# One attention-and-mixing kernel: a new planner for the work between the score steps, one four-bank score tile with one exp per step, and four small moves

## The chip, the cores and the metric

The kernel runs on one core of one Trainium2 chip. The metric is the device time of one execution in microseconds (us). An execution has a state: fast, or slow when it is over 1.5% above the fastest of the same kernel. A profile is of one execution. The engines are PE (TensorE; PEld is its weight load), ScalarE (ACT), VectorE (DVE), POOL (GpSimd), and SP, whose queue issues nearly all DMAs here.

## The reference

Two attention blocks on the same input of 2048 rows and 640 columns, 32 heads of 20 columns, mixed by a gate per row:

```python
g = sigmoid((x * gate_w).sum(-1))
a = A(x)    # linear attention: q,k -> softmax(+-(q @ w_phi)) features, num/den, @ wo
b = B(x)    # 4 segments of 512 rows: causal softmax attention inside a segment,
            # plus a memory M of the segments before it, mixed by sigmoid(beta), @ wo
return g * a + (1 - g) * b
```

## The kernel before

The first stage (about 97 us) builds the key side of block A and the first segment of block B. Then 32 iterations follow: four segments of eight groups of four heads. An iteration computes scores and exps for one group in three steps (t = 0, 1, 2; 2048, 2048 and 1024 exps per partition), and multiplies the probabilities of the group before with V:

```python
POFF = {0: 0, 1: 512, 3: 896, 2: 1024}
def b_qk(qT, kT, PT, cs):                       # one step
    st2 = [pst.tile([P, 2, 512], F32, name="st") for _ in range(2)]   # 2 x 2 banks, bufs=2
    base = POFF[cs[0]]
    for c in cs:
        ...
        for i in range(4):                      # four heads, 32 rows of the array each
            nc.tensor.matmul(st2[i // 2][:, i % 2, o:o + n], lhsT=kT[...], rhs=qT[...], ...)
    for pr in range(2):
        nc.scalar.activation(out=PT[:, 2 * pr:2 * pr + 2, base:base + w],
                             in_=st2[pr][:, :, 0:w], func=ACT.Exp, scale=SCALE_B)
```

All other work fills PE between these steps as *filler*: projections of the next segment's q, k, v (`b`, `v`), block A's query features (`p`), denominators (`d`) and numerators (`n`), and the output projections (`f`). The kernel is emitted by a planner in Python with a clock of its own: each unit yields the PE time it should take, and `later(dt, f)` emits an instruction dt after. Matmuls run in the order emitted, so a unit placed too early stops everything behind it: in the profile below PE stands 4.40 us before one projection's load, and ScalarE then waits 4.9 us for the scores behind it.

```python
def pick(at):                                   # at: position in iterations
    if BF and BF[0][0] <= at:                   # b, v, f units have a position
        return BF.pop(0)[1]()
    if A3:                                      # p, d, n: whenever nothing else is due
        return A3.pop(0)()
    if BF and BF[0][0] <= at + 1.0:
        return BF.pop(0)[1]()
    return None

ITER = 6.25
PART = (0.38, 0.37, 0.25)
t0 = clock[0]
for k in range(NG):                             # 32 iterations
    at = float(k)
    for t, cs in enumerate(((0,), (1, 3), (2,))):
        now, end = clock[0], t0 + ITER * (at - 0 + PART[t])   # a fixed, absolute timetable
        b_qk(qT, kT, PT, cs)
        while gets and gets[0][0] <= at:
            gets.pop(0)[1]()                    # transposing loads for the projections
        ...
        fill(end, at)
        at += PART[t]
```

An output projection needs its rows transposed. They are stored to DRAM (`od`), loaded transposed (`oT`), multiplied, cast to `osb` and stored to the output. All three DMAs go through SP's queue:

```python
def o_get(s, X, qc, n=KC):
    oT = bw.tile([P, KC, P], BF16, name=f"oT{X}", bufs=5)
    nc.sync.dma_start_transpose(out=oT[:, 0:n], in_=od[s][X][rows, 0:n * P])

def fin_mm(s, qc, hf, X):
    for k5 in range(KC):
        nc.tensor.matmul(sg.ps[:, 0:320], lhsT=sg.oT[qc, X][:, k5, :], rhs=(WoA, WoB)[X][...], ...)
        yield 0.137
    if X:
        nc.vector.tensor_copy(out=sg.osb[...], in_=sg.ps[:, 0:320])
        if hf:
            later(0.6, lambda: nc.sync.dma_start(out=out2[...], in_=osb))
```

The softmax here doesn't subtract the row's maximum and nothing guards it: scores larger than these inputs give would overflow.

## Time and profile before

The median is 378.41 us (four runs, 377.37 to 381.14). The profiled run is the slowest of these, 381.14 us by the run's clock and 379.4 us from first to last instruction. From the starts of the first exp of each iteration in ScalarE's timeline, the profiled 379.4 us split like this:

| stage | us | per iteration |
|---|---|---|
| to the first exp | 97.1 | |
| iterations 0 to 22 | 172.1 | 7.5 |
| iterations 23 to 30 | 82.0 | 10.3 |
| iteration 31 and tail | 28.2 | |

The page of the kernel before: busy tenths of PE in 40 slices of the span, and the clock granted to TensorE in tenths.

```profile
PE   7799998999899998869889899999869665688885
PEclk9999999999999989998899999999987985676597
```

Busy time by window; the columns after the window's length are PE, PEld, VectorE, ScalarE and POOL busy us (instructions), granted clock, DMA share, GB/s.

```profile
229.00:262.00 33.00, 32.42 (x462) 20.94 (x460) 23.81 (x68) 26.93 (x35) 16.73 (x25) 1.00 0.80 182
295.00:328.00 33.00, 20.18 (x239) 11.77 (x236) 13.46 (x36) 14.00 (x18) 17.04 (x28) 0.78 0.58 114
328.00:357.00 29.00, 22.97 (x269) 13.24 (x270) 8.20 (x23) 17.32 (x22) 11.28 (x18) 0.62 0.35 84
```

Where PE is full (229 to 262 us) an iteration takes about 6.6 us; later PE is idle a third of the time and what it does runs at a lower clock. The waits that matter (us in total, times, longest):

```profile
ACT PT L421 <- PE st L415: 66.9, 66, 4.9
PEld L595 <- DMA oT<-od: 13.0, 5, 4.9
PE o_ps L595 <- DMA oT<-od: 11.1, 4, 4.4
PE st L415 <- ACT PT L421: 6.5, 12, 0.9
```

PE's timeline in that stretch (start, us, instruction; idle time before it in brackets):

```profile
313.17 1.44 PE L595 MATMUL o_ps<-WoA,oT 128*128 128x320 bf16 x5 [3.37 <-DMA oT<-od]
319.56 1.25 PE L595 MATMUL o_ps<-WoB,oT 128*128 128x320 bf16 x4 [4.40 <-DMA oT<-od]
323.63 0.84 PE L595 MATMUL o_ps<-WoB,oT 128*128 128x320 bf16 x5
325.97 0.34 PE L415 MATMUL st<-qk 32*128 32x384 bf16 x2 [0.91 <-ACT PT L421]
326.88 0.59 PE L415 MATMUL st<-qk 32*128 32x384 bf16 x6 [0.58 <-ACT PT L421]
329.06 1.52 PE L595 MATMUL o_ps<-WoA,oT 128*128 128x320 bf16 x5 [1.59 <-DMA oT<-od]
```

```profile
295.72 1.42 SPq L401 DMA_TRANSPOSE qk<-qd  x1
302.54 0.33 SPq L604 DMA_DIRECT2D out_dram<-osb  x1
316.69 1.48 SPq L401 DMA_TRANSPOSE qk<-qd  x1
325.10 0.33 SPq L604 DMA_DIRECT2D out_dram<-osb  x1
325.54 2.52 SPq L585 DMA_TRANSPOSE oT<-od  x2
```

Five projection matmuls take 0.84 us at the full clock and 1.5 us after a stretch of waits.

### The profile page before, as it was taken

How to read it: one execution, taken by the hardware profiler on the slowest of the kernel's cores; microseconds unless marked ns; L12 is line 12 of the kernel's file. 1: busy time of each engine (PE TensorE's matmuls, PEld its weight loads, DVE VectorE, ACT ScalarE, POOL GpSimd, SP SyncE). 2: the span in 40 equal slices, each digit the busy share in tenths (PEclk: the TensorE clock that was granted, in tenths of full speed). 3: DMA queues.
4: the chain of work that ended last, by engine and by line, in shares of the span. 5: the costliest groups of instructions: out<-in, count | busy, mean ns of one | idle time of the engine just before them, and what ended most of it. 6: DMA issues, size and time to landing. Idle time of an engine off the chain costs nothing.

```text
span 379.4 us, 9867 instructions
## 1 busy us (share of the span) xinstructions
PE 326.8 (86%) x3999; PEld 210.0 (55%) x4015; DVE 234.8 (62%) x553; ACT 240.7 (63%) x394; POOL 202.7 (53%) x361
## 2 busy tenths in 40 slices
PE   7799998999899998869889899999869665688885
PEld 2577876775465556445556555666535442344462
DVE  1568788777496758666678866877654740233421
ACT  2476665543889868768778788878647452456510
POOL 3149995744484665964445485455564961333500
PEclk9999999999999989998899999999987985676597
DMA  9999200046262432447649487877454557414101
GB/s 187 189 172 363 67 3 2 6 186 175 52 140 86 148 80 97 102 130 173 172 82 192 131 120 218 176 171 137 146 127 146 84 152 136 93 38 118 42 15 56
DMA packets 98327, 46.55 MB, mean 123 GB/s; under 512 B 85482, under 2 KB 96234, under 8 KB 98282
## 3 DMA queue, kind: packets, MB, share of 16 engines
q1 hardware_dynamic: 96304, 45.08, 49.6%
q10 hardware_dynamic: 1978, 0.85, 0.9%
q8 instruction: 31, 0.51, 0.6%
q14 instruction: 14, 0.11, 0.1%
HBM read 4.95 MB, written 20.19 MB: 66 GB/s over the span
## 4 chain that ended last, share of the span: by engine, by line
PE 46%; DVE 19%; ACT 15%; DMA 7%; issue 4%; POOL 4%; SPq 4%; DVEq 0%; ACTq 0%; POOLq 0%
ACT PT L421 8%; PE o_ps L595 7%; PE st L415 7%; PE nd_ps L440 6%; PE qb_ps L230 4%; DVE ksum L262 4%; PE pq_ps L502 4%; PE vb_ps L230 4%; ACT Ek L257 4%; DMA oT<-od 3%; PE kb_ps L230 2%; PE o_ps L780 2%; PE va_ps L230 2%; DVE ts L561 2%; DVE krec L264 2%
## 5 line engine op out<-in xcount | busy, mean ns | idle before, releaser
L421 ACT ACTIVATE PT<-st 128x1024 bf16<-128x1024 f32 (+1 forms) x192 | 159.1, 885 | 68.2 <-PE st L415 66.9
L427 POOL TENSOR_SCALAR_AFFINE_SELECT PT<-PT 128x512 bf16<-128x512 bf16 x128 | 80.1, 640 | 96.3 <-ACT PT L421 96.1
L230 PEld LDWEIGHTS <-xT 128*128 128x128 bf16 x810 | 71.7, 98 | 36.5 <-issue 8.5
L440 PEld LDWEIGHTS <-PT 128*128 128x128 bf16 x1280 | 46.4, 98 | 13.2 <-issue 3.3
L415 PE MATMUL st<-qk 32*128 32x128 bf16 (+3 forms) x512 | 44.8, 326 | 7.6 <-ACT PT L421 6.5
L440 PE MATMUL nd_ps<-vB,PT 128*128 128x21 bf16 x1280 | 47.2, 174 | 0.5 <-DVE dz L525 0.4
L266 POOL TENSOR_TENSOR EkN<-Ek,krec 128x640 bf16<-128x640 bf16 x16 | 25.5, 1593 | 26.0 <-DVE krec L264 26.0
L595 PEld LDWEIGHTS <-oT 128*128 128x128 bf16 x240 | 21.4, 106 | 27.0 <-DMA oT<-od 13.0
L415 PEld LDWEIGHTS <-qk 32*128 32x128 bf16 x512 | 13.7, 93 | 39.1 <-issue 36.3
L502 PE MATMUL pq_ps<-xT,WqA 128*128 128x512 bf16 x84 | 29.3, 411 | 4.1 <-DVE ts L561 1.1
L569 POOL TENSOR_TENSOR oA<-ts 128x320 bf16<-128x320 f32 x32 | 27.6, 874 | 8.8 <-DVE ts L561 8.6
L595 PE MATMUL o_ps<-WoA,oT 128*128 128x320 bf16 x120 | 27.6, 350 | 5.0 <-DMA oT<-od 5.0
L595 PE MATMUL o_ps<-WoB,oT 128*128 128x320 bf16 x120 | 26.4, 328 | 6.2 <-DMA oT<-od 6.1
L475 DVE RECIPROCAL rd<-nd_ps 128x16 f32<-128x16 f32 x32 | 8.1, 254 | 36.9 <-PE nd_ps L440 33.2
L262 DVE TENSOR_REDUCE ksum<-Ek 128x64 f32<-128x1280 bf16 x16 | 23.8, 1485 | 10.8 <-ACT Ek L257 10.8
L556 PE MATMUL num_ps<-KVZ,Eq 128*128 128x140 bf16 (+1 forms) x192 | 20.0, 218 | 12.0 <-DVE stg L383 2.7
L230 PE MATMUL vb_ps<-WvB,xT 128*128 128x320 bf16 x160 | 29.9, 305 | 0.1
L230 PE MATMUL qb_ps<-WqB,xT 128*128 128x320 bf16 x160 | 29.8, 304 | 0.0
L230 PE MATMUL kb_ps<-WkB,xT 128*128 128x320 bf16 x160 | 29.2, 302 | 0.7 <-DVE stg L383 0.7
L257 ACT ACTIVATE Ek<-ka_ps 128x320 bf16<-128x320 f32 x64 | 23.0, 440 | 10.0 <-DVE krec L264 3.6
L561 DVE TENSOR_TENSOR ts<-num_ps,cs 128x320 f32<-128x320 f32 x64 | 27.6, 480 | 2.8 <-POOL cs L546 1.8
L600 DVE CAST osb<-o_ps 128x320 bf16<-128x320 f32 x24 | 11.6, 484 | 26.8 <-PE o_ps L595 26.8
(116 smaller groups left out, 539.2 us busy)
## 6 DMA issues: line engine op xcount, KB each, us to landing
qd<-stg SPq DMA_DIRECT2D x16, 768.0 KB, 3.8
od<-oA SPq DMA_DIRECT2D x16, 160.0 KB, 1.8
out_dram<-osb SPq DMA_DIRECT2D x15, 160.0 KB, 1.9
od<-oB SPq DMA_DIRECT2D x12, 160.0 KB, 1.9
WvA<-in_A_wqkv_dram ACTq DMA_DIRECT2D x2, 400.0 KB, 5.2
WkB<-in_B_wk_dram SPq DMA_DIRECT2D x1, 800.0 KB, 5.4
WqB<-in_B_wq_dram SPq DMA_DIRECT2D x1, 800.0 KB, 7.2
WvB<-in_B_wv_dram SPq DMA_DIRECT2D x1, 800.0 KB, 8.9
```

The lines of the kernel that those rows point to most:

```text
L230: nc.tensor.matmul(ps, lhsT=xT[:, c, sc * P:(sc + 1) * P], rhs=W[:, c, lo:hi], start=(c == 0), stop=(c == KC - 1))
L257: nc.scalar.activation(out=Ek[:, sgn, 320 * hf:320 * hf + 320], in_=ps[:, 0:320], func=ACT.Exp, scale=1.0 if sgn == 0 else -1.0)
L262: nc.vector.tensor_reduce(out=ksum, in_=Ek.rearrange("p s (h f) -> p (s h) f", f=DH), axis=AX.X, op=ALU.add)
L266: eng.tensor_tensor(out=EkNs[sc % 4][:, sgn * D:(sgn + 1) * D].rearrange("p (h f) -> p h f", f=DH), in0=Ek[:, sgn].rearrange("p (h f) -> p ...
L415: nc.tensor.matmul(st2[i // 2][:, i % 2, o:o + n], lhsT=kT[r:r + 32, c * P:(c + 1) * P], rhs=qT[r:r + 32, c * P:L], start=True, stop=True, ...
L421: nc.scalar.activation(out=PT[:, 2 * pr:2 * pr + 2, base:base + w], in_=st2[pr][:, :, 0:w], func=ACT.Exp, scale=SCALE_B)
L427: nc.gpsimd.affine_select(out=view, in_=view, pattern=[[0, 4], [1, P]], compare_op=ALU.is_ge, fill=0.0, base=0, channel_multiplier=-1)
L440: nc.tensor.matmul(nd[:, j * 84 + i * V1:j * 84 + (i + 1) * V1], lhsT=PT[:, i, o:o + P], rhs=vb[:, c, 4 * g + i, :], start=(j == 0 and i = ...
L502: nc.tensor.matmul(ps, lhsT=WqA[:, c, t * P:(t + 1) * P], rhs=xT[:, c, s * L:(s + 1) * L], start=(c == 0), stop=(c == KC - 1))
L561: nc.vector.tensor_tensor(out=ts[:, sgn], in0=ps[:, 0:320].rearrange("p (h e) -> p h e", e=DH), in1=segs[s].cs[hf][:, qc, sgn, :, None].to ...
L569: nc.gpsimd.tensor_tensor(out=oA[:, hf * 320:hf * 320 + 320].rearrange("p (h d) -> p h d", d=DH), in0=ts[:, 0], in1=ts[:, 1], op=ALU.add)
L595: nc.tensor.matmul(sg.ps[:, 0:320], lhsT=sg.oT[qc, X][:, k5, :], rhs=(WoA, WoB)[X][:, k5, hf * 320:hf * 320 + 320], start=(X == 0 and k5 = ...
```

## The change

The intent: keep PE, ScalarE and the DMA queue evenly loaded through all 32 iterations. The diff, cut to its core:

```diff
-        st2 = [pst.tile([P, 2, 512], F32, name="st") for _ in range(2)]
+        st = pst.tile([P, 4, 512], F32, name="st")          # one tile, four banks; bufs=2 -> 1
...
-        for pr in range(2):
-            nc.scalar.activation(out=PT[:, 2 * pr:2 * pr + 2, base:base + w],
-                                 in_=st2[pr][:, :, 0:w], func=ACT.Exp, scale=SCALE_B)
+        nc.scalar.activation(out=PT[:, :, base:base + w], in_=st[:, :, 0:w], func=ACT.Exp,
+                             scale=SCALE_B)
...
-            later(1.0, least)                               # feature map's min, behind its exp
+            later(2.2, least)
-            later(0.5 if s == 0 else 1.0, ...store of qd...)
+            later(0.5 if s == 0 else 2.2, ...)
-            later(1.0, invert)
+            later(1.7, invert)
-            nc.vector.tensor_tensor(out=Mbd[:, g], ...)
+            nc.gpsimd.tensor_tensor(out=Mbd[:, g], ...)
...
     for ic in range(KC):
         run(fold_mm(WkT, WkA, ic))
+        if ic == 2:
+            gate_column()                                   # was after a1_v(1)
...
+    KNOTS_A = ((0, 0.0), (0.37, 8.0), (0.54, 16.0), (0.69, 24.0), (1, 29.6))
+    KNOTS_F = ((0, 10.4), (0.21, 16.0), (0.44, 24.0), (0.64, 27.0), (1, 32.0))
+    # five lists b, v, p, n (with d), f; every unit has a position on these curves
+    def ready(u):
+        if u[0] == "d":   # 1.5 us after its exps
+        if u[0] == "n":   return now > done.get(("d", u[1], u[3]), 1e9) + 5.2
+        if u[0] == "f":   return now > got.get((u[1], u[2], u[4]), 1e9) + 4.5
+        ...
+    def pump(at):         # loads: position reached, data stored 2.2 us ago, a buffer free
...
     def pick(at):         # of the ready heads within 1.6 positions: the latest one,
+        ...               # minus HOLD x the planned backlog of the engines that it loads
...
-    t0 = clock[0]
     for k in range(NG):
+        t0 = clock[0]
+        size = OWN + left() / (NG - k)                      # budget from the work that is left
...
-            now, end = clock[0], t0 + ITER * (at - 0 + PART[t])
+            now, end = clock[0], t0 + size * (at - k + PART[t])
```

Three more `p` units also run before the loop (six instead of three).

More of the change, by code (lines that the diff above doesn't have):

```diff
@@ L74, with use @@
     waiting = []
+    load = {"D": 0.0, "A": 0.0, "G": 0.0, "S": 0.0}
+    def use(**cost):
+        for e, dt in cost.items():
+            load[e] = max(load[e], clock[0]) + dt
     serial = itertools.count()
@@ L388, in b_k @@
                 feature(stg[:, :, 0, :, 0:DH], pk[:, :, :, 0:DH])
-            later(0.5 if s == 0 else 1.0, lambda: nc.sync.dma_start(
+            later(0.5 if s == 0 else 2.2, lambda: nc.sync.dma_start(
                 out=qd[s][c * P:(c + 1) * P, :], in_=stg.rearrange("p g t i e -> p (g t i e)")))
@@ L414, in b_qk @@
                 r = 32 * i
-                nc.tensor.matmul(st2[i // 2][:, i % 2, o:o + n],
+                nc.tensor.matmul(st[:, i, o:o + n],
                                  lhsT=kT[r:r + 32, c * P:(c + 1) * P],
@@ L432, in b_qk @@
         later(1.7 if w > 256 else 1.0, causal)
+        use(A=1.7 if w > 256 else 0.95, G=0.65 * len(cs))
     def b_pv(s, g, PT, js, nd):
@@ L468, in b_mem @@
                                     in1=Msb[:, g], op=ALU.add)
-            nc.vector.tensor_tensor(out=Mbd[:, g], in0=Msb[:, g],
+            nc.gpsimd.tensor_tensor(out=Mbd[:, g], in0=Msb[:, g],
                                     in1=bd4[:, :, None].to_broadcast([P, 4, V1]), op=ALU.mult)
@@ L573, in add @@
                 later(1.0, lambda: o_put(s, 0, qc, oA))
-                if s == NSEG - 1:
-                    later(3.4, lambda: o_get(s, 0, qc))
         later(0.6, add)
+    put, got = {}, {}
     def o_put(s, X, qc, src, w=D):
         nc.sync.dma_start(out=od[s][X][qc * P:(qc + 1) * P, 0:w], in_=src[:, 0:w])
+        put[s, qc, X] = clock[0]
     def o_get(s, X, qc, n=KC):
@@ L586, in o_get @@
         segs[s].oT[qc, X] = oT
+        got[s, qc, X] = clock[0]
     def fin_mm(s, qc, hf, X):
@@ L604, in fin_mm @@
                 later(0.6, lambda: nc.sync.dma_start(out=out2[ch * P:(ch + 1) * P, :], in_=osb))
+    KNOTS_A = ((0, 0.0), (0.37, 8.0), (0.54, 16.0), (0.69, 24.0), (1, 29.6))
+    KNOTS_F = ((0, 10.4), (0.21, 16.0), (0.44, 24.0), (0.64, 27.0), (1, 32.0))
+    EARLY, HOLD, OWN, NEQ = 1.6, 1.5, 2.3, 6
     wps = wtile("warm_ps")
@@ L611 @@
         run(fold_mm(WkT, WkA, ic))
+        if ic == 2:
+            gate_column()
     run(a1_k(0))
     run(a1_v(1))
-    gate_column()
     run(gate_first())
@@ L640, in fill_a3 @@
     def fill_a3():
-        u = [("p", 0, 0), ("p", 0, 1), ("p", 0, 2), ("d", 0, 0), ("p", 0, 3), ("p", 0, 4)]
+        u = [("p", 0, t) for t in range(KC)] + [("p", 1, 0), ("d", 0, 0), ("d", 0, 1)]
         for s in range(NSEG):
             more = s + 1 < NSEG
-            u += [("n", s, 0, 0), ("n", s, 1, 0), ("d", s, 1), ("n", s, 2, 0), ("n", s, 3, 0)]
-            u += [("p", s + 1, 0), ("p", s + 1, 1)] * more
+            u += [("n", s, 0, 0), ("n", s, 1, 0)]
+            u += [("d", s, 1)] * (s > 0)
+            u += [("n", s, 2, 0), ("n", s, 3, 0)]
+            u += [("p", s + 1, 1), ("p", s + 1, 2)] * more
@@ L646, in fill_a3 @@
             u += [("n", s, 0, 1), ("n", s, 1, 1)]
-            u += [("p", s + 1, 2), ("d", s + 1, 0)] * more
+            u += [("d", s + 1, 0)] * more
             u += [("n", s, 2, 1), ("n", s, 3, 1)]
             u += [("p", s + 1, 3), ("p", s + 1, 4)] * more
-        fn = {"p": a3_pq, "d": a3_den, "n": a3_num}
-        return [lambda v=v: fn[v[0]](*v[1:]) for v in u]
-    def fill_fin(s, p0, p1):
-        u = [(qc, hf, X) for qc in range(4) for hf in range(2) for X in range(2)]
-        out = [(p0 + (p1 - p0) * i / 16, lambda v=v: fin_mm(s, *v)) for i, v in enumerate(u)]
-        return out, [(p0 + (p1 - p0) * qc / 4 - 0.95 + 0.25 * X,
-                      lambda qc=qc, X=X: o_get(s, X, qc)) for qc in range(4) for X in range(2)]
@@ L659 @@
-    A3 = fill_a3()
-    BF, gets = [], []
-    for s in range(1, NSEG):
-        BF += fill_bkv(s)
-    for s, (p0, p1) in enumerate(((10.4, 18.4), (18.6, 26.4), (26.5, 31.6))):
-        f, g = fill_fin(s, p0, p1)
-        BF += f
-        gets += g
-    BF.sort(key=lambda v: v[0])
-    gets.sort(key=lambda v: v[0])
+            u += [("p", s + 2, 0)] * (s + 2 < NSEG)
+        return u
+    COST = {"p": 1.09, "d": 0.65, "n": 0.39, "b": 0.69, "v": 0.69, "f": 0.69}
+    USE = {"p": {"A": 1.25}, "d": {"D": 0.8, "G": 1.7}, "n": {"D": 0.8, "G": 0.87},
+           "b": {"D": 0.4}, "v": {"D": 0.4}, "f": {}}
@@ new lines, with place @@
+    done = {}
+    def place(units, knots):
+        total = sum(COST[u[0]] for u in units)
+        out, x = [], 0.0
+        for u in units:
+            for (x0, p0), (x1, p1) in zip(knots, knots[1:]):
+                if x / total <= x1:
+                    break
+            out.append((p0 + (p1 - p0) * (x / total - x0) / (x1 - x0), u))
+            x += COST[u[0]]
+        return out
+    a3 = fill_a3()
+    first, a3 = a3[0:6], place(a3[6:], KNOTS_A)
+    lists = {"p": [v for v in a3 if v[1][0] == "p"], "n": [v for v in a3 if v[1][0] != "p"]}
@@ new lines @@
+    lists["b"], lists["v"] = [], []
+    for s in range(1, NSEG):
+        lists["b"] += place([("b", s, c, f, hf) for c in range(4) for f in range(2)
+                             for hf in range(2)], ((0, 8 * s - 8), (1, 8 * s - 2.0)))
+        lists["v"] += place([("v", s, c, 2, hf) for c in range(4) for hf in range(2)],
+                            ((0, 8 * s - 6.6), (1, 8 * s - 0.1)))
+    lists["f"] = place([("f", s, qc, hf, X) for s in range(NSEG - 1) for qc in range(4)
+                        for hf in range(2) for X in range(2)], KNOTS_F)
@@ new lines @@
+    import os
+    DBG = os.environ.get("DBG")
+    ATT=[0.0]
+    POS = {u: p for key in lists for p, u in lists[key]}
+    gets = []
+    for p, (_, s, qc, hf, X) in lists["f"]:
+        if hf == 0:
+            gets.append((p - 1.4, s, qc, X))
+    gets += [(29.0, NSEG - 1, qc, X) for qc in range(4) for X in (1, 0)]
+    def ready(u):
+        now = clock[0]
+        if u[0] == "p":
+            n = 5 * u[1] + u[2] - NEQ
+            return n < 0 or ("n", n // 5, 3, int(n % 5 > 1)) in done
+        if u[0] == "d":
+            return all(now > done.get(("p", u[1], t), 1e9) + 1.5
+                       for t in ((0, 1, 2), (2, 3, 4))[u[2]])
+        if u[0] == "n":
+            return now > done.get(("d", u[1], u[3]), 1e9) + 5.2
+        if u[0] == "f":
+            return now > got.get((u[1], u[2], u[4]), 1e9) + 4.5
+        if u[0] == "v" and u[1] > 1:
+            return (u[1] - 2, G - 1) in done
+        if u[0] == "b" and 1 < u[1] < NSEG - 1 and u[3] == 1:
+            return ("mem", u[1] - 2, G - 1) in done
+        return True
@@ new lines, in start, with finish @@
+    def start(u):
+        if u[0] in "bv":
+            return (b_q, b_k, b_v)[u[3]](u[1], u[2], u[4])
+        return {"p": a3_pq, "d": a3_den, "n": a3_num, "f": fin_mm}[u[0]](*u[1:])
+    def finish(u):
+        done[u] = clock[0]
+        if DBG: print(f"{u} want {POS.get(u,0):.2f} at {ATT[0]:.2f}")
+        cost = dict(USE[u[0]])
+        if u[0] == "f" and u[4]:
+            cost = {"D": 0.4}
+        if u[0] == "b" and u[3] < 2 and u[4] and (u[3] == 0 or u[1] < NSEG - 1):
+            cost = {"D": 1.35, "A": 0.7}
+        use(**cost)
@@ L670 @@
+    def pump(at):
+        while gets and gets[0][0] <= at and load["S"] <= clock[0]:
+            _, s, qc, X = gets[0]
+            n = 4 * s + qc - 5
+            if clock[0] < put.get((s, qc, X), 1e9) + 2.2:
+                return
+            if n >= 0 and ("f", n // 4, n % 4, 1, X) not in done:
+                return
+            gets.pop(0)
+            o_get(s, X, qc, 3 if s == NSEG - 1 and X else KC)
+            use(S=1.3)
     run(a1_kv(NCH - 2))
@@ L682 @@
     psa_stack.close()
-    pst = ctx.enter_context(tc.tile_pool(name="pst", bufs=2, space=PSUM, reuse_waits="tile"))
+    pst = ctx.enter_context(tc.tile_pool(name="pst", bufs=1, space=PSUM, reuse_waits="tile"))
     bw = ctx.enter_context(tc.tile_pool(name="bw", bufs=2, reuse_waits="tile"))
@@ L691 @@
             gates()
-        if c > 0:
-            run(A3.pop(0)())
+        for u in first[0:2] if c > 0 else ():
+            run(start(u))
+            finish(u)
+            first.remove(u)
     while not segs[0].first:
@@ L700, in pick @@
     def pick(at):
-        if BF and BF[0][0] <= at:
-            return BF.pop(0)[1]()
-        if A3:
-            return A3.pop(0)()
-        if BF and BF[0][0] <= at + 1.0:
-            return BF.pop(0)[1]()
-        return None
+        best = None
+        for key in "bfnpv":
+            if not lists[key]:
+                continue
+            p, u = lists[key][0]
+            if p > at + EARLY or not ready(u):
+                continue
+            late = (at - p) * (3.0 if key == "b" else 1.0)
+            if late > 1.0:
+                late += 4.0 if key == "b" else 1.0
+            for e, dt in USE[u[0]].items():
+                late -= HOLD * max(0.0, load[e] - clock[0] - 0.9)
+            if best is None or late > best[0]:
+                best = (late, key)
+        if best is None:
+            return None
+        return lists[best[1]].pop(0)[1]
     def fill(until, at):
         while clock[0] < until - 0.05:
+            pump(at)
             if unit[0] is None:
-                unit[0] = pick(at)
-                if unit[0] is None:
+                u = pick(at)
+                if u is None:
                     return
-            dt = next(unit[0], None)
+                unit[0] = (u, start(u))
+            dt = next(unit[0][1], None)
             if dt is None:
+                finish(unit[0][0])
                 unit[0] = None
@@ L719, in fill, with left @@
                 tick(dt)
-    ITER = 6.25
+    def left():
+        return sum(COST[u[0]] for key in lists for _, u in lists[key])
     PART = (0.38, 0.37, 0.25)
@@ L734 @@
         at = float(k)
+        ATT[0]=at
+        t0 = clock[0]
+        size = OWN + left() / (NG - k)
         for t, cs in enumerate(((0,), (1, 3), (2,))):
-            now, end = clock[0], t0 + ITER * (at - 0 + PART[t])
+            now, end = clock[0], t0 + size * (at - k + PART[t])
             b_qk(qT, kT, PT, cs)
-            while gets and gets[0][0] <= at:
-                gets.pop(0)[1]()
+            pump(at)
             if t == 0 and k + 1 < NG:
@@ L747 @@
                     run(b_mem(ps_, pg_, pphi, res))
+                    done["mem", ps_, pg_] = clock[0]
+                    use(D=0.85 * (ps_ > 0) + 0.2, G=0.3)
                 elif t == 1:
@@ L758 @@
                     b_epi(ps_, pg_, nd, res["tm"], oB)
+                    done[ps_, pg_] = clock[0]
+                    use(D=0.85, G=0.87)
                     if pg_ == G - 1:
@@ L764 @@
                                                   for qc in range(4)])
-                        for qc in range(4):
-                            later(5.0 + 1.3 * qc, lambda qc=qc: o_get(last, 1, qc, 3))
             fill(end, at)
             at += PART[t]
+            ATT[0]=at
         prev = (s, g, PT, phiq)
@@ L771 @@
             cur = nxt
-    while unit[0] is not None or A3 or BF:
+    while unit[0] is not None or left() > 0 or gets:
         fill(clock[0] + 1.0, NG)
+        tick(0.05)
     def tail_a(qc, o2):
@@ L800, in tail_b @@
             nc.sync.dma_start(out=rows, in_=osb)
-    def pair():
-        st = pst.tile([P, 2, 512], F32, name="st")
-        return [st[:, hf, 0:320] for hf in range(2)]
     tail = {}
@@ L813 @@
     run(b_pv(last, pg_, pPT, [0, 1], nd))
-    run(tail_a(1, pair()))
+    st = pst.tile([P, 4, 512], F32, name="st")
+    run(tail_a(1, [st[:, hf, 0:320] for hf in range(2)]))
     run(b_pv(last, pg_, pPT, [2, 3], nd))
@@ L817 @@
     b_epi(last, pg_, nd, res["tm"], oB)
-    run(tail_a(2, pair()))
+    run(tail_a(2, [st[:, 2 + hf, 0:320] for hf in range(2)]))
     tp = wtile("otp", BF16)
```

## The prediction

> **What bounds it now.** The busy-time windows and the timeline of ScalarE split the 379.4 us span in three: a first stage to 97 us, 32 attention iterations from the first exp at 97.1 to 357 us, and a tail of 22.4 us. The iterations average 8.1 us, but unevenly. Iterations 17 to 22 take 6.55 us each with PE busy 32.4 of 33 us (229 to 262 us): PE-bound. The last nine, 269 to 357 us, take 9.8 us each. There PE is busy only 20.2 of 33 us (295 to 328), and the waits view shows PE and its weight loads waiting 24 us for the transposing DMA oT<-od. The instruction order says why: after iteration 26 the list of A work is used up, and only output-projection units are left, each behind its DMA. The granted clock falls with it, 0.78 and then 0.62: five o_ps matmuls take 1.5 us there, about 0.85 us at full clock. That idleness costs clock is what the Trainium skill, "TensorE: Matmul & The Clock Gate" (What's actually happening), says; this trace agrees.
>
> **What the change does.**
> 1. It spreads the filler evenly. Weighting each matmul kind with its full-clock spacing, filler per iteration is now 4.0 us up to iteration 26, then 3.5, 2.1, 2.1, 1.4; after the change the order shows 3.4 to 3.9 us nearly everywhere to iteration 30, with projections behind guards for their DMA. Cost with about 2.5 us of attention: 6.0 us of PE per iteration. This should remove most of the late 25 us of PE idling and the slow clock.
> 2. One exp over four banks in place of two over two banks. From 605 ns (512 columns) and 1026 ns (1024) I estimate 1.87 us for 2048, so ScalarE saves only about 0.2 us per iteration. But the score tile now has one buffer: QK waits for the whole exp. My estimate of the chain, scores 0.4 to 0.5 us plus exp 1.87, 1.87 and 1.03 plus hand-overs, is 6.4 to 6.5 us, more than PE's 6.0; Eq and ek exps in ScalarE's queue (about 1.1 us per iteration) push it on. I expect about 7.0 us per iteration. This takes back part of the gain: PE's waits for PT exps rise from 6.5 us to 15 to 35 us in total.
> 3. gate_column earlier: removes the 2.45 us PE wait for WvA before g_ps at 14.9 us; about 2 us gained.
> 4. 24 Mbd products (401 ns each on VectorE) go to POOL, which has room (about half busy): under 1 us. Three more pq units before the loop cost about 3 us there, mostly taken from inside it. Some projections are left for after the loop: the tail grows to about 25 us.
>
> **Sum.** First stage 97 (minus 2, plus 3, rounded), 32 x 7.15 = 229, tail 25: 351 us; I say 352 us, range 338 to 368. Chances: faster by over 2% 0.88, within 2% 0.08, slower by over 2% 0.04.
>
> **What would show it.** Spacing of iterations nearly uniform at 6.6 to 7.4 us; waits for oT<-od below 8 us; granted clock above 0.9 between 285 us and the loop's end; no g_ps wait; exp of 2048 columns at 1.8 to 1.9 us; POOL carrying Mbd.
>
> **What would make it wrong.** If hand-overs of the single score buffer cost more than 1.5 us per iteration, gain shrinks below 5%. If VectorE or POOL queues hold PSUM tiles back (waits of PE for ts, stg or osb above 20 us), likewise. If ScalarE's other exps fit into the hand-over gaps and PE stays the limit at 6.2 us, it lands near 325 us.

## The result, and the profile after

The changed kernel takes 338.97 us (median of 11 runs, 337.17 to 341.06); the kernel before 378.05 us (16 runs). The ratio is 0.8959 (95% interval 0.893 to 0.8988). A ratio is the mean time of one kernel's fast runs over that of the other's fast runs of the same rounds, so not quite the ratio of the medians. The two profiled executions lie at opposite ends of their runs (381.14 and 336.91 us), so the gains by stage add up to 44.2 us and not to the 39 us between the medians.

| stage | before, us | after, us | gain |
|---|---|---|---|
| to the first exp | 97.1 | 97.1 | 0.0 |
| iterations 0 to 22 | 172.1 | 157.1 | 15.0 |
| iterations 23 to 30 | 82.0 | 55.0 | 27.0 |
| iteration 31 and tail | 28.2 | 26.0 | 2.2 |
| span of the profile | 379.4 | 335.2 | 44.2 |

Iterations now average 6.84 us and lie between 6.2 and 7.95. The page's rows of the changed kernel, its windows and its waits:

```profile
PE   7999998999998898988999989999988987899974
PEclk9999999999999999999999999999999999999999
```

```profile
229.00:262.00 33.00, 29.78 (x467) 19.82 (x465) 24.37 (x64) 24.16 (x17) 22.60 (x39) 1.00 0.74 168
295.00:315.00 20.00, 18.39 (x290) 12.16 (x287) 14.71 (x39) 14.75 (x10) 16.96 (x29) 1.00 0.55 138
```

```profile
ACT PT L426 <- PE st L421: 37.7, 62, 2.1
PE st L421 <- ACT PT L426: 9.7, 32, 0.7
```

PE's wait for the loads has gone from the loop (1.3 us are left in the tail), the clock is full throughout, and ScalarE's longest wait for scores is 2.1 us instead of 4.9. The exps, by shape, before and after:

```profile
L421 ACT ACTIVATE PT<-st 128x1024 bf16<-128x1024 f32 x128 | 124.3, 1026 | 49.2 <-PE st L415 48.0 <-POOL PT L427 0.9
L421 ACT ACTIVATE PT<-st 128x512 bf16<-128x512 f32 x64 | 35.1, 605 | 19.0 <-PE st L415 18.9
```

```profile
L426 ACT ACTIVATE PT<-st 128x2048 bf16<-128x2048 f32 x64 | 120.3, 1879 | 30.4 <-PE st L421 27.4 <-POOL PT L432 1.4 <-POOL oA L575 1.3
L426 ACT ACTIVATE PT<-st 128x1024 bf16<-128x1024 f32 x32 | 32.8, 1026 | 10.3 <-PE st L421 10.3
```

The merged exp of 2048 columns takes 1879 ns against an estimate of 1.87 us. The Trainium skill, "ScalarE: Activation LUTs" (Rules for kernel authors), gives about 0.83 ns per element and 0.3 us per instruction whose bias is a pointer operand. For immediate scale and bias, which these exps have in the built program, the same page (What ACT_TABLE_LOAD costs) gives 186 ns as the fixed part. These rows give (1879 - 1026) / 1024 = 0.83 ns per column and 0.17 us fixed, so the slope agrees and the fixed part is close to the second figure. The merge saves 159.4 - 153.1 = 6.3 us of ScalarE in all.

### The profile page after: what moved, and what is told of

Its sections match the earlier page's. It is cut to its first block, busy times and chain, and to the rows that moved or that the text cites. A ratio compares the mean times of both kernels' runs of the same rounds, so it can differ in the third digit from the quotient of the medians.

```text
span 335.2 us, 9765 instructions
## 1 busy us (share of the span) xinstructions
PE 299.9 (89%) x4000; PEld 202.4 (60%) x4015; DVE 229.3 (68%) x529; ACT 234.6 (70%) x298; POOL 211.8 (63%) x385
## 4 chain that ended last, share of the span: by engine, by line
ACT 31%; PE 30%; DVE 17%; DMA 7%; POOL 6%; issue 4%; SPq 3%; ACTq 0%; DVEq 0%; POOLq 0%
ACT PT L426 21%; PE st L421 5%; DVE ksum L268 4%; ACT Ek L263 4%; PE pq_ps L508 3%; PE nd_ps L446 3%; PE qb_ps L236 3%; DMA qk<-qd 2%; PE va_ps L236 2%; DMA oT<-od 2%; PE kb_ps L236 2%; PE o_ps L603 2%; ACT Eq L513 2%; ACT ek L375 2%; ACT Eq L512 2%
## 5 line engine op out<-in xcount | busy, mean ns | idle before, releaser
L426 ACT ACTIVATE PT<-st 128x2048 bf16<-128x2048 f32 (+1 forms) x96 | 153.1, 1595 | 40.7 <-PE st L421 37.7
L432 POOL TENSOR_SCALAR_AFFINE_SELECT PT<-PT 128x512 bf16<-128x512 bf16 x128 | 81.7, 651 | 37.3 <-ACT PT L426 37.2
L236 PEld LDWEIGHTS <-xT 128*128 128x128 bf16 x810 | 69.6, 97 | 34.8 <-issue 9.0
L421 PE MATMUL st<-qk 32*128 32x128 bf16 (+3 forms) x512 | 34.7, 300 | 12.5 <-ACT PT L426 9.7
L508 PE MATMUL pq_ps<-xT,WqA 128*128 128x512 bf16 x85 | 24.6, 380 | 3.4 <-DVE td L485 1.0
L236 PE MATMUL va_ps<-WvA,xT 128*128 128x320 bf16 (+1 forms) x160 | 24.8, 299 | 1.4 <-DVE gl L249 0.9
L603 PEld LDWEIGHTS <-oT 128*128 128x128 bf16 x240 | 18.9, 97 | 9.9 <-issue 4.9
L603 PE MATMUL o_ps<-WoA,oT 128*128 128x320 bf16 x120 | 24.4, 299 | 0.0
L236 PE MATMUL ka_ps<-WkA,xT 128*128 128x320 bf16 x160 | 24.3, 298 | 0.0
L603 PE MATMUL o_ps<-WoB,oT 128*128 128x320 bf16 x120 | 24.2, 299 | 0.0
```

What stands on the lines that cost most here:

```text
L236: nc.tensor.matmul(ps, lhsT=xT[:, c, sc * P:(sc + 1) * P], rhs=W[:, c, lo:hi], start=(c == 0), stop=(c == KC - 1))
L421: nc.tensor.matmul(st[:, i, o:o + n], lhsT=kT[r:r + 32, c * P:(c + 1) * P], rhs=qT[r:r + 32, c * P:L], start=True, stop=True, tile_positio ...
L426: nc.scalar.activation(out=PT[:, :, base:base + w], in_=st[:, :, 0:w], func=ACT.Exp, scale=SCALE_B)
L432: nc.gpsimd.affine_select(out=view, in_=view, pattern=[[0, 4], [1, P]], compare_op=ALU.is_ge, fill=0.0, base=0, channel_multiplier=-1)
L508: nc.tensor.matmul(ps, lhsT=WqA[:, c, t * P:(t + 1) * P], rhs=xT[:, c, s * L:(s + 1) * L], start=(c == 0), stop=(c == KC - 1))
```

## The experiments

Twelve kernels ran. The theory I started with, called A: the gain came from spreading the filler, while the single score buffer costs. I compare ratios to the kernel before. All results were correct.

| label | what | median, us | ratio to before | 95% interval |
|---|---|---|---|---|
| (changed kernel) | | 338.97 | 0.8959 | 0.893 to 0.8988 |
| e1_two_bufs | changed, score tile and exp split again | 339.56 | 0.9012 | 0.897 to 0.9055 |
| e2_merge_only | before + one tile, one exp | 378.92 | 1.0031 | 0.9968 to 1.0093 |
| e3_pace_only | before + positions | 377.83 | 1.0016 | 0.9965 to 1.0067 |
| e4_gate_only | before + early gate column | 374.26 | 0.9927 | 0.9885 to 0.9969 |
| e11_more_bufs | before + 8 load buffers | 378.62 | 1.0019 | 0.9983 to 1.0055 |
| e10_early_gets | before + earlier loads | 366.78 | 0.9717 | 0.9685 to 0.9748 |
| e9_f_guard_off | changed, projection guard off | 343.55 | 0.9078 | 0.903 to 0.9127 |
| e8_a_guards_off | changed, A margins and engine weights off | 340.03 | 0.902 | 0.8975 to 0.9065 |
| e12_pace_guard | before + positions + loads and guard | 382.97 | 1.0122 | 1.0082 to 1.0162 |
| e14_fixed_budget | changed, old timetable | 380.03 | 1.0064 | 1.0022 to 1.0106 |
| e13_old_delays | changed, old delays | 342.73 | 0.9069 | 0.9037 to 0.9101 |
| e15_tail_order | changed, tail reordered | 338.72 | 0.8964 | 0.8933 to 0.8996 |

### The score tile and the merged exp (e1, e2)

e1 is the changed kernel with these lines undone; e2 is the kernel before with them alone.

```diff
+        st2 = [pst.tile([P, 2, 512], F32, name="st") for _ in range(2)]   # bufs=2
-        st = pst.tile([P, 4, 512], F32, name="st")                        # bufs=1
```

> The changed kernel with the score tile split again into two two-bank halves and two exps per step, everything else (order of PE work, placement, guards) kept. Theory A (the single four-bank buffer costs hand-overs, 0.50 + 0.39 + 0.56 us of ScalarE idling per iteration in the chain; the gain came from the even placement of filler): ScalarE's waits for scores (37.7 us) fall by 10 us or more and the kernel gets faster, 325 to 335 us. Rival B (the merged exp is a part of the gain): ScalarE needs about 0.2 us more per iteration, 6 us, and the kernel is slower, 343 to 350 us. If neither matters: 337 to 341 us.

> The kernel before with only the score tile and exp changed: one four-bank buffer, one exp. The old filler list and order stay. Theory A: no gain, 376 to 392 us, since the late starvation stays and hand-overs are added; PE's waits for the exps rise from 6.5 us to 10 us or more. Rival B: 360 to 372 us.

Neither way moves the time clearly: e2's interval includes 1, and e1's overlaps the changed kernel's. e1's profile shows why. This is PE's wait for exps there, and ScalarE's group:

```profile
PE st L421 <- ACT PT L427: 2.7, 8, 0.5
L427 ACT ACTIVATE PT<-st 128x1024 bf16<-128x1024 f32 (+1 forms) x192 | 158.8, 887 | 36.8 <-PE st L421 34.7
```

Two buffers cut PE's wait by 9.7 - 2.7 = 7.0 us; two exps cost ScalarE 158.8 - 153.1 = 5.7 us. The two effects are of one size. The Trainium skill, "Perfetto Trace Analysis" (Optimizing Scalar/DVE Operations), says that larger operations help where an engine is saturated, and that breaking up instructions may help where they cause bubbles on other engines; here ScalarE is not saturated (busy 172 of 212 us of the changed kernel's loop), both effects are there, and the time does not move. That they cancel is a reading of the two sums, not shown apart from them. Theory A's part on the single buffer falls, and so does rival B. (e2's profiled run was a slow one.)

### The gate column alone (e4)

```diff
         run(fold_mm(WkT, WkA, ic))
+        if ic == 2:
+            gate_column()
     run(a1_k(0))
     run(a1_v(1))
-    gate_column()
```

> The kernel before with only the gate column made earlier, after the third fold. The 2.45 us wait of PE before g_ps goes. If the first stage is a chain of PE and VectorE work, the whole 2.0 to 2.4 us shows: 375.5 to 376.5 us. If the start of the iterations hangs on the DMA of qd and qk (9 us before the first exp) and slack exists before it, less than 0.7 us shows.

The ratio is 0.9927, about 2.8 us of 377.3, interval 1.2 to 4.3. The wait is gone; here is `g_ps` in the kernel before and then in e4 (idle time in brackets):

```profile
17.32 0.40 PE L230 MATMUL g_ps<-WvA,xT 128*128 128x1 bf16 x10 [2.45 <-DVE WvA L324]
```

```profile
13.99 0.39 PE L230 MATMUL g_ps<-WvA,xT 128*128 128x1 bf16 x10
93.75 1.95 ACT L421 ACTIVATE PT<-st 128x1024 bf16<-128x1024 f32 x2
```

The loop starts at 93.75 us instead of 97.09. In the changed kernel it starts at 97.06 again: the time went into the three extra `p` units before the loop.

### Positions alone (e3)

The kernel before with A work and projections on the changed kernel's curves and a simple rule, in place of "A work whenever nothing is due":

```diff
-        if BF and BF[0][0] <= at: ...
-        if A3: return A3.pop(0)()
+        head = min((v for v in (BF, A3) if v), key=lambda v: v[0][0], default=None)
+        if head is None or head[0][0] > at + 1.0:
+            return None
+        return head.pop(0)[1]()
```

> The kernel before with only the filler placed at the changed kernel's positions (A work spread to position 29.6, projections to 32, earliest position first), without readiness guards, without engine loads, with the old two score buffers and two exps. Theory A: most of the 27 us that the last nine iterations gave come back: 345 to 358 us, and waits for the transposing DMA of the projections under 10 us instead of 24. Rival C (placement alone is worth little; the guards and loads that order units by what is ready are what matters): 362 to 378 us.

It gained nothing: 377.83 us. PE still waits for oT (12.4 us on the weight loads), and two iterations between 283.7 and 305.2 us take 10.2 and 11.3 us. Theory A, as "these positions alone are the gain", falls. Evenness itself was not tested by it: its iterations still lie between 6.2 and 11.6 us (spacing of their first scores). The number fits rival C, and the next runs ask which of its parts.

### Why the loads come late (e11, e10)

Two explanations of the late waits for `oT`. D1: the last segment's four A tiles are loaded early and hold four of five buffers until the tail. D2: the loads come too late in SP's queue, behind the store of `osb`.

```diff
-        oT = bw.tile([P, KC, P], BF16, name=f"oT{X}", bufs=5)
+        oT = bw.tile([P, KC, P], BF16, name=f"oT{X}", bufs=(8, 5)[X])        # e11
```

```diff
-        return out, [(p0 + (p1 - p0) * qc / 4 - 0.95 + 0.25 * X,
+        return out, [(p0 + (p1 - p0) * qc / 4 - 2.2 + 0.25 * X, (s, X, qc),  # e10
...
-            while gets and gets[0][0] <= at:
+            while gets and gets[0][0] <= at and clock[0] > put.get(gets[0][1], 1e9) + 2.2:
```

> The kernel before with 8 instead of 5 buffers for the A half of the projection's transposed input; the order of instructions is the same on every engine. Theory D1 (the late stall is a shortage of these buffers: the four A tiles of the last segment are loaded early, stay until the tail and hold four of five, so that each load of segment 2 waits for the matmuls of the one before): waits for oT<-od fall from 24 us to under 10 and the kernel takes 355 to 368 us. Rival D2 (the loads are issued too late in the queue, whatever the buffers): 375 to 379 us. Rival of both (uneven filler and idling as such, my forecast's step 1): no change either.

> The kernel before with the transposing loads of the projections issued 1.25 iterations earlier than now (but not before their data has been stored), five buffers as before. D2 (issue too late): 358 to 370 us and waits for oT<-od under 10 us. D1 (buffers held): 373 to 380 us, waits still 15 us or more, since the loads of segment 2 are held by the buffers and not by their place.

D1 falls: with more buffers and the same order of instructions nothing changes. D2 holds as far as lateness goes: with earlier loads PE's waits for `oT` vanish from the list, and 2.8% (about 10.7 us) comes back. That a waiting store is what makes them late is read from the queue above, not tested alone. Its iterations 23 to 30 take 68.3 us (before 82.0, changed 55.0), its first 23 as long as before. The Trainium skill, "DMA: Bandwidth & Descriptors" (Anatomy of one DMA — SWDGE (gpsimd) path), says that any semaphore wait of a DMA happens on the issuing sequencer. The trace agrees for SP's queue, and shows the consequence: a store that waits holds up each load behind it (6.9 us idle in the queue above). So late loads are one part, and some 28 of 39 us are still open.

### Guards, weights and delays, taken out of the changed kernel (e9, e8, e13)

```diff
-            return now > got.get((u[1], u[2], u[4]), 1e9) + 4.5      # e9
+            return now > got.get((u[1], u[2], u[4]), 1e9)
-    EARLY, HOLD, OWN, NEQ = 1.6, 1.5, 2.3, 6                         # e8
+    EARLY, HOLD, OWN, NEQ = 1.6, 0.0, 2.3, 6
-            return ... done.get(("p", u[1], t), 1e9) + 1.5 ...       # e8
+            return ... done.get(("p", u[1], t), 1e9) ...
-            return now > done.get(("d", u[1], u[3]), 1e9) + 5.2      # e8
+            return now > done.get(("d", u[1], u[3]), 1e9) + 2.75
-            later(2.2, least) ... 2.2, store of qd ... 1.7, invert   # e13
+            later(1.0, least) ... 1.0 ... 1.0
```

(The delays inside a denominator add up to 0.5 + 1.7 + 0.5 = 2.7 us; 2.75 us is just long enough that its result is emitted before the numerators that read it.)

> The changed kernel with the guard of the projections taken off: a projection may be placed as soon as its load is issued, not 4.5 us later. If that guard is what removed the waits for the transposing DMA: waits for oT<-od (1.2 us now) rise to 10 us or more, and 348 to 362 us. If the early loads and the order of buffers suffice: 337 to 343 us.

> The changed kernel without the weighing of engine loads and with the waits between A units cut (denominator right after its exps, numerator 2.75 us after the denominator instead of 5.2); guard of the projections kept. If ordering by what is ready on VectorE, POOL and ScalarE made the 15 us gained in the first 23 iterations: 348 to 358 us, with more PE waits for ts, cs and Eq. If it is worth little: 337 to 342 us.

> The changed kernel with the old delays: the min of the feature map enqueued 1.0 us after its exp instead of 2.2, the store of qd 1.0 instead of 2.2, the reciprocal of the denominators 1.0 instead of 1.7. VectorE waited 7.1 us for ek before and 2.7 us after, 3.8 us for rr before. If VectorE blocked at the head of its queue held PE's PSUM tiles: 342 to 348 us. Otherwise 338 to 340 us.

Each is worth about 1%: 1.2 points of ratio for the projection guard, 1.1 for the delays, 0.6 for margins and weights (that interval overlaps the changed kernel's). One of e9's four runs was slow. In e9 the waits for oT come back in part, 5.8 us on the weight loads. In e13 VectorE's waits for the feature exp in the loop are 9.3 us instead of 1.7, as the theory of a blocked VectorE queue has it. None explains 28 us.

### Positions with guarded loads, and the timetable (e12, e14)

e12 adds to e3 the changed kernel's loads and projection guard. e14 is the changed kernel with the old timetable, and nothing else:

```diff
     prev = None
+    t0 = clock[0]
     for k in range(NG):
...
-        t0 = clock[0]
-        size = OWN + left() / (NG - k)
...
-            now, end = clock[0], t0 + size * (at - k + PART[t])
+            now, end = clock[0], t0 + 6.25 * (at + PART[t])
```

> The kernel before with the changed kernel's positions (as in the placement-only run, which gained nothing) and with the changed kernel's handling of the projections: loads issued when their data is stored and a buffer is free, projections placed only 4.5 us after their load. Still one fixed budget of 6.25 us per iteration, two score buffers, old delays, late gate column. If late loads were all that spoiled the placement-only run: 345 to 360 us, waits for oT<-od under 6 us. If the lumpy filling that remains (0 to 5.9 us of filler per iteration by the instruction order, against 3.4 to 3.9 in the changed kernel) costs as much again: 360 to 374 us.

> The changed kernel with one edit: the old fixed budget of 6.25 us per iteration counted from the start of the loop, in place of a budget recomputed for each iteration from the work that is left. Positions, guards, loads, one score buffer are kept. The instruction order then has 0 to 6.7 us of filler per iteration instead of 3.4 to 3.9. If evenness from iteration to iteration is what the schedule gains by: an iteration takes the longer of about 6.4 us (scores and exps) and 2.5 us plus its filler; summing what lies above 3.9 us of filler gives about 16 us, so 350 to 360 us. If evenness is worth little once loads are on time: 337 to 343 us.

e12 missed both its ranges: 382.97 us, although no wait of PE for `oT` is left in its list. So in the kernel before, rival C's guards and loads on top of the positions gain nothing either. And e14 loses everything: 380.03 us, ratio 1.0064. The budget rule, three lines of planning, is worth 11 points once the rest is there. By stage, e14's first 23 iterations take 176.4 us (changed kernel 157.1), iterations 23 to 30 take 72.0 us (55.0), and the rest 32.3 us (26.0). The waits of e14, which stand against 37.7 and 9.7 us in the changed kernel:

```profile
ACT PT L426 <- PE st L421: 70.1, 75, 5.0
PE st L421 <- ACT PT L426: 39.9, 44, 2.2
```

Both engines wait more for each other, in turns. PE's timeline of e14 around one lump, with ScalarE's:

```profile
305.76 0.61 PE L421 MATMUL st<-qk 32*128 32x384 bf16 x8 [1.46 <-ACT PT L426]
306.88 1.53 PE L603 MATMUL o_ps<-WoB,oT 128*128 128x320 bf16 x5
308.21 1.54 PE L603 MATMUL o_ps<-WoA,oT 128*128 128x320 bf16 x5
309.55 1.54 PE L603 MATMUL o_ps<-WoB,oT 128*128 128x320 bf16 x5
312.95 0.29 PE L421 MATMUL st<-qk 32*128 32x256 bf16 x4
318.46 0.60 PE L421 MATMUL st<-qk 32*128 32x384 bf16 x8 [1.24 <-ACT PT L426]
324.99 0.40 PE L421 MATMUL st<-qk 32*128 32x384 bf16 x8 [1.46 <-ACT PT L426]
```

```profile
306.42 1.88 ACT L426 ACTIVATE PT<-st 128x2048 bf16<-128x2048 f32 x1 [0.71 <-PE st L421]
313.29 1.02 ACT L426 ACTIVATE PT<-st 128x1024 bf16<-128x1024 f32 x1 [4.99 <-PE st L421]
```

Between two score steps PE does 6.6 us of other work, mostly filler, while ScalarE stands still for 4.99 us; in the next iteration there is hardly any filler and PE waits for exps, and the projections run at the lower clock (1.53 us for five). A unit that is held back by a guard or by its position leaves a hole in the plan. The fixed timetable is absolute, so the missed time is made up at once, as a lump, when units become ready. The recomputed budget starts from where the plan is and spreads what is left over all remaining iterations. The kernel before could live with the fixed timetable because its A list was never held back: it filled every hole until it ran out at iteration 26.

e14 changes two things at once, though: where the budget is counted from, and its size. 6.25 us is more than there is work for: the changed kernel's plan advances by 5.8 us per iteration on average. The planner is Python and its order can be built without a chip. Built so and not run, e14 with 5.8 in place of 6.25 plans 3.4 to 3.8 us of filler in iterations 1 to 30, as even as the changed kernel; with 6.25 us counted from each iteration's own start, iterations down to 0 us remain but none above 4.3 us. So in the plan the holes come from a budget that is too large, and the lumps from counting it absolutely. Without a run this says nothing of their times; a fixed timetable of the right size stays an untested rival to the recomputed budget.

Weighting each matmul of the instruction order with the time that the planner gives it, the filler per iteration and the measured length:

| e14: filler of the iteration | iterations | mean filler, us | mean length, us |
|---|---|---|---|
| under 2.9 us | 10 | 1.5 | 7.3 |
| 3.4 to 4.3 us | 11 | 4.0 | 7.5 |
| over 4.3 us | 10 | 5.3 | 9.3 |

In the changed kernel iterations 1 to 30 all have 3.4 to 3.9 us of filler and average 6.86 us. The short ones of e14 don't get shorter than the changed kernel's even ones, probably since the chain of scores and exps sets their length, and the long ones get much longer. The middle group takes 7.5 us with hardly more filler than the changed kernel has, so the amount of an iteration is not the whole of it.

### An attempt at a better one (e15)

```diff
-    for qc in range(3):
-        tail_b(qc)
+    tail_b(0)
     run(tail_a(3, ...))
-    tail_b(3)
+    for qc in range(1, 4):
+        tail_b(qc)
```

> An attempt to beat both: the changed kernel with the last row chunk's sixteen projection matmuls (2.2 us) placed after the first chunk's finish instead of after the third's, where PE waits 0.5 to 0.7 us four times for evacuations. If PE's work is what ends the tail: 1 to 2 us faster, 337 to 338 us. If the evacuations or the output DMA end it: no change.

No change: 0.8964 against 0.8959. The 2.2 us of matmuls are earlier, but the three remaining finishes still follow one another with waits of 0.5 to 0.7 us for evacuations. No version beat the changed kernel.

## Why the prediction was right or wrong

The time, 338.97 us, lies in the range of 338 to 368 close to its low end, and faster was given 0.88. Point by point:

1. *"It spreads the filler evenly ... This should remove most of the late 25 us of PE idling and the slow clock."* Right in what happens: iterations 23 to 30 went from 82.0 to 55.0 us and the clock is full. The cause was given too simply. "After iteration 26 the list of A work is used up" is true, but about 10.7 us of the late loss was loads issued too late (e10). And the positions that I took for the evening-out are worth nothing under the fixed timetable (e3, e12): what makes the filler even in this kernel is the recomputed budget (e14), which the prediction doesn't name. Nor does it name the other side of spreading: the first 23 iterations got 15.0 us shorter too, with filler of 4.0 us before and 3.4 to 3.9 us after by its own count. e14 loses that gain as well; it was not tested alone. My "24 us" of waits for oT was also a misreading: it adds two rows that wait side by side.
2. *"I expect about 7.0 us per iteration"*, 7.15 in the sum. This term was mis-sized: 6.84 us. The estimate of the chain, 6.4 to 6.5 us, was near (the shortest iterations take 6.2 to 6.4). Its sign, a spacing of 6.6 to 7.4 us, was missed at both ends (6.2 to 7.95). What I added for the other exps in ScalarE's queue was too much, and *"PE's waits for PT exps rise from 6.5 us to 15 to 35 us"* failed: 9.7 us. In the chain, a step hands over with ScalarE idle for 0.4 to 0.7 us, and the Eq and ek exps fall partly into such gaps. *"This takes back part of the gain"* was not shown: e1 and e2 are neutral.
3. *Gate column, "about 2 us gained"*: 2.8 us alone, interval 1.2 to 4.3 (e4), spent again on the three `p` units as forecast. First exp at 97.06 us; the forecast's terms give 98, rounded to 97 in its sum.
4. *Mbd on POOL*: 24 times 341 ns there instead of 401 ns on VectorE; not tried alone.
5. *"The tail grows to about 25 us."* Mis-sized: counted from the start of iteration 31, the sum had 7.15 + 25 = 32.2 us and the trace has 26.0. "Some projections are left for after the loop" failed: the trace has none there. And five tail matmuls take 0.84 us throughout, where the kernel before needed 1.54 us for three of its eight fives and 1.35 us for a fourth; I carried over the old tail's clock. How the 6.2 us divide between the two is open.

The time fell into the range because the range was wide; the sum of 351 us was 12 us too long. From iteration 0 to the end the sum was too long by 31 x (7.15 - 6.84) = 9.6 us and by 6.2 us of tail. The expectation of e14 itself was too small: a rule of "the longer of 6.4 us and 2.5 us plus filler" gave about 16 us, and 41 us were lost. The rule leaves out lumps within an iteration, between two score steps, and the lower clock after waits. How the 41 us divide among these causes is open. Also open: the size of the budget against where it is counted from (above), and the recomputed budget alone in the kernel before, which was not run, so nothing here says what it would do there.

## What to carry to other kernels

When filler work is planned between the steps of a chain, give each step a budget that fits the work that is left. Recomputing it does that by itself; the fixed one here was larger than the work and counted absolutely, so units that were held back returned as lumps, and with the lumps two engines waited in turns. A fixed budget of the right size was not run. The parts of such a change don't add up one by one, so take parts out of the new kernel as well as adding them to the old one; alone, none gained over 3% here, and one rule taken out lost all of it. Before shifting loads, look at what stands in front of them in the queue that issues them.

## What the Trainium skill lacked or had wrong

- "TensorE: Matmul & The Clock Gate" (HAM oscillation — how this bites in real kernels) warns of PE-idle gaps over about 3.4 us. Shorter ones did it here: in the kernel before, five projection matmuls took 0.84 us at 323.63 us and 1.52 us at 329.06 us, with gaps of 0.91, 0.58 and 1.59 us between them; in e14, where no listed wait of PE in the loop exceeds 2.2 us, the granted clock averages 0.69 to 0.84 in four windows of the loop. The page's next section (A second HAM failure mode: psum-queue depth-cycling) does say that frequent short idling makes the clock swing, but gives no length of gaps for it.
- "Perfetto Trace Analysis" (Optimizing Scalar/DVE Operations) gives both advices, larger instructions where the engine is saturated and smaller ones where it is not, but not what to expect of them: 7.0 us of PE's waits against 5.7 us of ScalarE's time here, and no clear difference in the kernel.
- "DMA: Bandwidth & Descriptors" says where a DMA's semaphore wait takes place; none of the pages that I used says what it costs the DMAs behind it in the queue. Here a waiting store left the queue without an issue for 6.9 us, and loads issued earlier gained 10.7 us.
